# First transfers cut into halves on two queues, and re-measured durations in the plan that orders a gated-attention and expert kernel

## The chip, the cores and the metric

The kernel runs on 1 core of a Trainium2 chip. The metric is the time of one execution in device microseconds (us), and the number to predict is the median of several runs.

## The reference, cut to what matters

A gated linear attention is followed by a two-level expert layer. The attention carries a 48x48 state per batch and head through 768 tokens; the expert layer sends each of the 3072 tokens to one of 16 experts, chosen first by group and then within the group.

```python
# attention: 4 batches, 8 heads, 768 tokens, 48 wide
state = np.zeros((B, H, D, D), dtype=np.float32)
for t in range(S):
    state = alpha[:, :, t, :, None] * state + np.einsum('bhd,bhe->bhde', k[:, :, t], v[:, :, t])
    y[:, :, t] = np.einsum('bhd,bhde->bhe', q[:, :, t], state)
...
x = np.ascontiguousarray(attn_out.transpose(0, 2, 1, 3)).reshape(B * S, H * D)
# experts: x is 3072 x 384; w1 16 x 384 x 1024; w2 16 x 1024 x 384
g_idx = np.argmax(x @ w_group, axis=1)
...
e_idx = np.argmax(xg @ w_expert[g], axis=1)
h = np.maximum(xg[mask_e] @ w1[g, e], 0.0)
out[tok_idx] = combined[:, None] * (h @ w2[g, e])
```

## The kernel before

The attention works on 24 chunks of 128 tokens (6 chunks for each of 4 batches), all eight heads of a chunk at a time, as four pairs in 112 of the 128 partitions. For each chunk n there is a chain of steps. The plan names them as follows, and the profile shows them by these lines.

- `load n`: one DMA of the chunk's decays, keys, queries and values (L463), on SP's queue. Of chunks 0, 1 and 2 the parts are loaded apart: `decay0` and `decay_0` (the two halves of chunk 0's decays), `key_0`, `query_0`, `decay1`, `key_1`, `query_1`, `decay2`, then `value0`, `load2`, `value1`. Four of them go over the ACT engine's queue.
- `rev n`: a scan of the decays backward on DVE (L469, tile kd); `turn n`: a reciprocal (L475); `forth n`: a scan forward (L480, tile cq).
- `key n` and `query n`: products with keys and queries on POOL (L485 and L489, tile in or w).
- `score n`: the score matmuls on PE (L503, tile zs), masked by DVE (L512) or by an ACT copy (L517) and a POOL cut (L520).
- `turn_k n` and `kept n`: keys transposed on PE (L532, into tile zo), copied out by ACT (L537). `gain n`: matmuls (L545). `grow n`: DVE adds the old state (L554, tile sums). `scale n+1`: four ACT operations (L558, tile state).
- `own_out n` and `from n`: the output matmuls (L569, L578, tile zo); `copy n`: ACT copies them out (L584, tile yt). There is one zo tile, so `turn_k n`, which writes into it, waits for `copy n-2`.
- `row n`: matmuls (L592) that give the token rows and the expert logits. For every six chunks of the first three batches, DVE chooses the experts (from L612 to L697), and POOL sends each chunk's rows to DRAM with an indirect DMA, `scatter n` (L746).

After the attention come 18 jobs of the expert layer, with their matmuls on L281; they take the rest of the time.

What runs on each engine in which order is not written out by hand. `Plan` holds every step with its engine, a duration in us, its predecessors, and for a transfer the time from its end to its landing. `Plan.order` simulates the engines with these numbers, takes at each point the ready step with the longest remaining path, and the steps are then emitted in that order; each engine executes its list strictly in that order, whatever the real times are:

```python
soonest = max(free[e], min(early[n] for n in names))
near = [n for n in names if early[n] <= soonest + patience]
n = max(near, key=lambda m: level[m] - 2.0 * max(0.0, early[m] - soonest))
```

`warm` issues matmuls on a constant tile before the first real ones; `WARM` has their numbers (27 before chunk 0's scores, 5 behind them).

Of the kernel before, what the change touches and what calls it, by code (L numbers as in the profile page):

```python
# [19 lines left out]
ENG = mybir.EngineType  # L20
# [3 lines left out]
P = 128  # L24
# [3 lines left out]
class Plan:  # L28

    LAG = {ENG.PE: 0.2, ENG.DVE: 0.1, ENG.Activation: 0.2, ENG.Pool: 0.12, ENG.SP: 0.1}  # L30
# [80 lines left out]
def gla_then_hierarchical_moe(  # L111
# [32 lines left out]
    nc = tc.nc  # L144
# [3 lines left out]
    R = 64 + D  # L148
# [232 lines left out]
    with ExitStack() as gla:  # L381
# [323 lines left out]
        def add_send(g, b, c0, c1, counted, weighed, after_scatter):  # L705
# [51 lines left out]
            for c in range(C):  # L757
# [3 lines left out]
                plan.add(f"scatter{t0 + c}", POOL, 1.28, partial(scatter, c),  # L761
# [30 lines left out]
        WARM = (27, 5)  # L792
# [75 lines left out]
        begin("query_0", True, 0, KQ, VW)  # L868
        begin("decay1", False, 1, 0, AW)
        begin("key_1", True, 1, AW, KQ)  # L870
        begin("query_1", False, 1, KQ, VW)
        begin("decay2", True, 2, 0, AW)
        begin("value0", False, 0, VW, IW)
        begin("load2", False, 2, AW, IW)
        begin("value1", False, 1, VW, IW)
        begin("load3", False, 3)
# [38 lines left out]
        def add_decays(n):  # L915
# [6 lines left out]
            for i, (p0, p1) in enumerate(c.back):  # L922
                k = p1 - p0
                add(f"rev{n}.{i}", DVE, 0.13 + 0.273 * k, partial(back, c, p0, p1),
                    after=[src[0] if i == 0 else "decay_0", *prev, *free,
                           f"scale{n - 4}.{HP - 1}"])
                add(f"key{n}.{i}", POOL, 0.15 + 0.27 * k, partial(keys, c, p0, p1),
                    after=[f"rev{n}.{i}", src[1]])
            add(f"turn{n}", DVE, 0.18, partial(turn, c, 0, HP), after=ends_of(n, "rev", c.back))
            for i, (p0, p1) in enumerate(c.forth):  # L930
                k = p1 - p0
                add(f"forth{n}.{i}", DVE, 0.13 + 0.273 * k, partial(forth, c, p0, p1),
                    after=[f"turn{n}"])
                add(f"query{n}.{i}", POOL, 0.15 + 0.27 * k, partial(queries, c, p0, p1),
                    after=[f"forth{n}.{i}", src[2]])

        def add_scores(n):
# [8 lines left out]
            for i in range(2):  # L946
                if i < on_vector:
                    add(f"mask{i}.{n}", DVE, 0.69, partial(mask_all, c, i),
                        after=[f"score{n}", "causal", late(n - 2, "own_out")])
                    made["masked", n, i] = f"mask{i}.{n}"  # L950
                else:
                    add(f"mask{i}.{n}", ACT, 0.58, partial(mask_copy, c, i),
# [8 lines left out]
        def add_turned(n):  # L961
# [6 lines left out]
            add(f"kept{n}", ACT, 0.54, partial(kept_keys, c),  # L968
                after=[f"turn_k{n}", late(n - 2, "gain")])

        def add_rows(n):
            c = chunks[n]
            PEQ(f"row{n}", 0.87, partial(to_rows, c), after=[f"copy{n}", "wr"],
                reader=f"logit{n}")
            if in_bulk(n):
                add(f"kept_r{n}", ACT, 0.49, partial(kept_rows, c), after=[f"row{n}"])
                add(f"logit{n}", ACT, 0.25, partial(kept_logits, c), after=[f"row{n}"])
            else:
                add(f"logit{n}", DVE, 0.23, partial(logits, c), after=[f"row{n}"])
                add(f"kept_r{n}", ACT, 0.49, partial(kept_rows, c), after=[f"logit{n}"])  # L980
# [5 lines left out]
        def add_gains(n):  # L986
# [5 lines left out]
            if c.bc:  # L992
                add(f"grow{n}", DVE, 0.35, partial(grown, c),
                    after=[f"gain{n}", f"scale{n}.3", late(n - 1, "scale") and f"scale{n - 1}.3"])
            for p in range(HP):
                add(f"scale{n + 1}.{p}", ACT, 0.32, partial(scaled, chunks[n + 1], p),
# [3 lines left out]
        def add_outputs(n):  # L1000
            c = chunks[n]
            PEQ(f"own_out{n}", 0.99, partial(outputs, c),
# [4 lines left out]
            add(f"copy{n}", ACT, 0.58, partial(copied, c),  # L1007
# [368 lines left out]
    kept = []  # L1376
# [129 lines left out]
```

## Time and profile before

| what | value |
|---|---|
| median of 3 runs | 381.13 us (380.58 to 381.78) |
| the profiled execution, as timed | 380.29 us |
| its span in the profile | 378.6 us |
| PE busy, share of the span | 368.6 us, 97% |
| attention, from the first score matmul to the last job's preparation | about 7 to 122 us of the span |

The profiled execution is one run; its time is 1.69 us more than its span, and 0.84 us less than the median. PE is the engine that sets the pace; of the idle time of the others only that matters which makes PE wait.

### The profile page before, as it was taken

To read this page: it belongs to the slowest core of one execution; us is meant where nothing else is said; L and a number is where in the kernel's file an instruction comes from. 1 tells how busy PE (TensorE), PEld (TensorE's weight loads), DVE (VectorE), ACT (ScalarE), POOL (GpSimd) and SP (SyncE) were. 2 spreads that over 40 slices of the span, in tenths; PEclk is the share of its full clock that TensorE was granted. 3 is DMA by queue.
4 is the path that set the end of the run, shared out by engine and by line. 5 is a ranking of instruction groups with operands and counts; after the bars stand their busy time and mean duration, and the time that the engine had idled before them with its cause. 6 is when DMAs were issued, how large, how long until landed. Compare 5 with 4: busy or idle time off the path is not lost.

```text
span 378.6 us, 10166 instructions
## 1 busy us (share of the span) xinstructions
PE 368.6 (97%) x4122; PEld 350.4 (93%) x4122; DVE 156.7 (41%) x346; ACT 119.2 (31%) x315; POOL 200.3 (53%) x241
## 2 busy tenths in 40 slices
PE   8899999999999999999999999999999999999994
PEld 5788888888789999999999999999999999999983
DVE  6799999898976301209402022020220211201200
ACT  2666766777553121111112121121211212211210
POOL 5988779889886023526254261633525426236251
PEclk9999999999999999999999999999999999999999
DMA  8999997879883699999676576866868657655001
GB/s 291 386 402 395 410 404 259 264 249 368 317 267 131 210 331 366 348 362 344 254 227 219 190 239 242 282 217 204 243 240 294 218 197 275 260 197 192 8 22 37
DMA packets 30930, 98.08 MB, mean 259 GB/s; under 512 B 18056, under 2 KB 20036, under 8 KB 26275
## 3 DMA queue, kind: packets, MB, share of 16 engines
q1 hardware_dynamic: 25523, 86.95, 65.3%
q0 software_dynamic: 4784, 9.55, 7.4%
q10 hardware_dynamic: 576, 0.92, 0.7%
q8 instruction: 33, 0.54, 0.6%
q14 instruction: 14, 0.11, 0.1%
HBM read 85.76 MB, written 12.07 MB: 258 GB/s over the span
## 4 chain that ended last, share of the span: by engine, by line
PE 90%; POOL 3%; issue 2%; DVE 2%; DMA 1%; SPq 0%; POOLq 0%; ACT 0%; DVEq 0%
PE bank L281 63%; PE zs L503 5%; PE bank L592 5%; PE zo L569 5%; PE zo L578 3%; PE bank L545 2%; PE zs L281 2%; PE zo L532 2%; PE bank L1362 2%; DMA in<-in_rows_dram 1%; POOL in L489 1%; DVE kd L469 1%; POOL slots_d L746 1%; DVE cq L480 1%; POOL in L485 0%
## 5 line engine op out<-in xcount | busy, mean ns | idle before, releaser
L1197 POOL DMA_INDIRECT out_dram<-yq,dst_q x98 | 95.1, 971 | 146.5 <-DVE yq L1193 110.8
L281 PE MATMUL bank<-hT,w 128*64 128x96 f32 (+14 forms) x768 | 117.5, 318 | 0.0
L281 PEld LDWEIGHTS bank<-hT,w 128*128 128x128 f32 (+1 forms) x768 | 115.4, 184 | 0.0
L281 PE MATMUL bank<-xt_e,w 128*64 128x120 f32 (+14 forms) x816 | 113.5, 311 | 0.0
L281 PEld LDWEIGHTS bank<-xt_e,w 128*128 128x128 f32 (+1 forms) x816 | 111.6, 178 | 0.2 <-issue 0.2
L1240 DVE SCALAR_TENSOR_TENSOR dst_q<-xq,past_q 128x7 int32<-128x7 int32 (+1 forms) x13 | 2.2, 166 | 146.9 <-DMA out_dram<-yq,dst_q 146.9
L297 ACT ACTIVATE hT<-bank 128x192 f32<-128x192 f32 (+15 forms) x68 | 32.0, 470 | 94.8 <-PE bank L281 94.8
L308 ACT COPY yT<-bank 128x192 f32<-128x192 f32 (+28 forms) x30 | 11.9, 395 | 101.4 <-PE bank L281 101.4
L746 POOL DMA_INDIRECT slots_d<-xr,place x24 | 24.1, 1004 | 6.9 <-issue 3.8
L592 PE MATMUL bank<-wr,yt 112*64 112x116 f32 x384 | 25.3, 266 | 0.0
L1190 DVE STREAM_TRANSPOSE yq<-yT 128x672 f32<-128x672 f32 (+2 forms) x16 | 12.6, 788 | 20.2 <-ACT yT L308 20.2
L592 PEld LDWEIGHTS bank<-wr,yt 112*64 112x64 f32 x384 | 20.4, 137 | 0.4
L485 POOL TENSOR_TENSOR in<-in,kd 112x512 f32<-112x512 f32 (+1 forms) x15 | 16.7, 1116 | 5.1 <-DMA in<-in_rows_dram 2.8
L503 PE MATMUL zs<-in 48*64 48x128 f32 (+1 forms) x352 | 16.0, 275 | 2.8 <-POOL in L489 2.8
L520 POOL TENSOR_SCALAR_AFFINE_SELECT sm<-sm 128x512 f32<-128x512 f32 x27 | 16.7, 635 | 3.3 <-ACT sm L517 3.1
L584 ACT COPY yt<-zo 112x512 f32<-112x512 f32 x24 | 14.0, 585 | 14.0 <-PE zo L578 11.5
L558 ACT ACTIVATE state<-sums,kd 112x48 f32<-112x48 f32 x64 | 17.8, 331 | 1.7 <-DVE sums L554 1.7
L469 DVE TENSOR_TENSOR_SCAN kd<-in,starts 112x516 f32<-112x516 f32 (+1 forms) x15 | 17.0, 1138 | 2.9 <-DMA in<-in_rows_dram 2.8
L517 ACT COPY sm<-zs 128x512 f32<-128x512 f32 x27 | 15.4, 590 | 8.3 <-PE zs L503 7.6
L503 PEld LDWEIGHTS zs<-in 48*64 48x64 f32 (+1 forms) x352 | 13.4, 148 | 4.7 <-POOL in L489 4.0
L480 DVE TENSOR_TENSOR_SCAN cq<-in,starts 112x516 f32<-112x516 f32 (+1 forms) x16 | 17.2, 1088 | 0.8
L489 POOL TENSOR_TENSOR in<-in,cq 112x512 f32<-112x512 f32 (+1 forms) x16 | 16.9, 1060 | 0.9 <-DVE cq L480 0.7
(161 smaller groups left out, 406.9 us busy)
## 6 DMA issues: line engine op xcount, KB each, us to landing
w<-in_w_dram SPq DMA_DIRECT2D x36, 1536.0 KB, 7.1
in<-in_rows_dram SPq DMA_DIRECT2D x11, 962.5 KB, 10.4
w<-in_rows_dram SPq DMA_DIRECT2D x10, 962.5 KB, 14.5
xq<-slots_d SPq DMA_DIRECT2D x28, 85.8 KB, 9.5
slots_d<-blank SPq DMA_DIRECT2D x2, 980.0 KB
xq<-slots_d SPq DMA_DIRECT2D x24, 73.5 KB, 5.1
out_dram<-yq,dst_q POOLq DMA_INDIRECT x98
in<-in_rows_dram SPq DMA_DIRECT2D x1, 704.0 KB
```

The lines of the kernel that those rows point to most:

```text
L281: nc.tensor.matmul(z[s], lhsT=w[:, s], rhs=x, start=first, stop=last, skip_group_check=True)
L297: nc.scalar.activation(out=hT[:, f0:f0 + 2, 0:n], in_=z[:, 0:2 * n].rearrange("p (f t) -> p f t", f=2), func=AF.Relu)
L469: nc.vector.tensor_tensor_scan(out=flat(c.kd[:, p0:p1])[:, ::-1], data0=c.t[0:R, A1 * p1:A1 * p0:-1], data1=one_col.to_broadcast([R, A1 * ...
L480: nc.vector.tensor_tensor_scan(out=flat(c.cq[:, p0:p1]), data0=c.t[0:R, A1 * p0:A1 * p1], data1=starts[0:R, A1 * p0:A1 * p1], initial=1.0, ...
L485: nc.gpsimd.tensor_tensor(out=c.k[:, p0:p1], in0=c.k[:, p0:p1], in1=c.kd[:, p0:p1, 1:A1], op=ALU.mult)
L489: nc.gpsimd.tensor_tensor(out=c.q[:, p0:p1], in0=c.q[:, p0:p1], in1=c.cq[:, p0:p1, 1:A1], op=ALU.mult)
L503: nc.tensor.matmul(c.zs[i][s, p, :], lhsT=c.k[r, p, s], rhs=c.q[r, p, :], start=True, stop=True)
L558: nc.scalar.activation(out=c.st[:, p, 0:D], in_=chunks[c.n - 1].sums[:, p], func=AF.Copy, scale=c.kd[:, p, 0:1])
L569: nc.tensor.matmul(of(c.zo, p)[o], lhsT=c.v[:, h * D:h * D + o.stop - o.start], rhs=c.sm[:, i, p, :], start=(p < 2), stop=(c.bc == 0), ski ...
L592: nc.tensor.matmul(z[s, p * W:(p + 1) * W], lhsT=c.yt[:, p, s], rhs=wr[:, p, :], start=True, stop=True)
L746: sent = nc.gpsimd.indirect_dma_start(out=slots_by[t], out_offset=bass.IndirectOffsetOnAxis(ap=m["place"][:, c:c + 1], axis=0), in_=xr[:, ...
L1197: nc.gpsimd.indirect_dma_start(out=out_by.popleft().rearrange("n (j w) -> (n j) w", j=4), out_offset=bass.IndirectOffsetOnAxis(ap=dst[:, b ...
```

## The change

Three things change. The first eleven transfers are issued as two DMAs each, partitions 0 to 63 on SP's queue and the rest on ACT's queue, one transfer behind the other in order of use; of those with decays, keys and queries only the 112 partitions in use are loaded (before: 128). The durations and lags in the plan get other numbers. The number of warming matmuls ahead of chunk 0's scores is 24 instead of 27. What each step computes is as it was.

```diff
-    LAG = {ENG.PE: 0.2, ENG.DVE: 0.1, ENG.Activation: 0.2, ENG.Pool: 0.12, ENG.SP: 0.1}
+    LAG = {ENG.PE: 0.2, ENG.DVE: 0.18, ENG.Activation: 0.28, ENG.Pool: 0.2, ENG.SP: 0.1}
...
-                plan.add(f"scatter{t0 + c}", POOL, 1.28, partial(scatter, c),
+                plan.add(f"scatter{t0 + c}", POOL, 1.1, partial(scatter, c),
...
-        WARM = (27, 5)
+        WARM = (24, 5)
...
-        def begin(name, by_act, n, a=0, b=IW):
-            add(name, SP, (b - a) * P * 4 / 383.0 / 1e3,
-                partial(load, chunks[n], a, b, nc.scalar if by_act else nc.sync),
-                row="sp", lands=0.3)
+        def begin(name, n, a, b, used=P):
+
+            def halves():
+                c = chunks[n]
+                home(c)
+                for eng, z in ((nc.sync, slice(0, 64)), (nc.scalar, slice(64, used))):
+                    eng.dma_start(out=c.t[z, a:b], in_=in_d[n, z, a:b])
+
+            add(name, SP, (b - a) * used * 4 / 400.0 / 1e3, halves, row="sp", lands=0.6)
...
-        begin("decay0", False, 0, 0, HW)
-        begin("decay_0", True, 0, HW, AW)
-        begin("key_0", False, 0, AW, KQ)
...
+        begin("decay0", 0, 0, HW, R)
+        begin("decay_0", 0, HW, AW, R)
+        begin("key_0", 0, AW, KQ, R)
...
-        begin("load3", False, 3)
+        dma("load3", 0.45, partial(load, chunks[3]), IW * 512, lands=0.6)
...
-                add(f"rev{n}.{i}", DVE, 0.13 + 0.273 * k, partial(back, c, p0, p1),
+                add(f"rev{n}.{i}", DVE, 0.05 + 0.273 * k, partial(back, c, p0, p1),
```

Fourteen more durations of the plan change in the same way, twelve of them downward (an ACT copy from 0.58 to 0.48, a scale from 0.32 to 0.235).

How the queues begin, in the order of the two programs. SP's queue before, with the waits on the counters of earlier transfers (DMAHW0 to DMAHW7):

```order
L463 DMA in<-in_rows_dram 128x259
L463 DMA in<-in_rows_dram 128x512
L463 DMA in<-in_rows_dram 128x517
L463 DMA in<-in_rows_dram 128x512
L463 DMA in<-in_rows_dram 128x384 [waits DMAHW0_49]
L463 DMA in<-in_rows_dram 128x1408 [waits DMAHW1_49]
```

ACT's queue after; SP's has the same list with 64 partitions in each row, and from its fifth row on such a wait too:

```order
L864 DMA in<-in_rows_dram 48x259
L864 DMA in<-in_rows_dram 48x258
L864 DMA in<-in_rows_dram 48x512 x2
L864 DMA in<-in_rows_dram 48x517 [waits DMAHW0_49]
L864 DMA in<-in_rows_dram 48x512 [waits DMAHW2_49]
L864 DMA in<-in_rows_dram 48x512 [waits DMAHW4_49]
L864 DMA in<-in_rows_dram 48x517 [waits DMAHW6_49]
L864 DMA in<-in_rows_dram 64x384 [waits DMAHW0_49]
L864 DMA in<-in_rows_dram 64x1408 [waits DMAHW2_49]
L517 ACT_TABLE_LOAD
L517 COPY sm<-zs_200 128x512 [waits PE_49]
L537 COPY kt<-zo 128x448 [waits PE_49]
```

ACT issued four transfers ahead of its table load before, and now ten; eight counters are shared by both queues, so that a ninth transfer waits for the first one's landing, as before. An eleventh, chunk 1's values, stands behind the two copies.

DVE at chunks 3 and 4, before (kd<-w_2_281 is `rev4`, which reads what `load4` brings; sums is `grow1`):

```order
L480 SCALAR_TENSOR_TENSOR cq<-in,starts 112x516
L554 TENSOR_TENSOR sums<-state_122,bank 112x192
L469 SCALAR_TENSOR_TENSOR kd<-w_2_281,starts 112x516
L475 RECIPROCAL starts<-kd 112x4
L480 SCALAR_TENSOR_TENSOR cq<-w_2_281,starts 112x516
```

The same place after:

```order
L480 SCALAR_TENSOR_TENSOR cq<-in,starts 112x516
L469 SCALAR_TENSOR_TENSOR kd<-w_2_285,starts 112x516
L554 TENSOR_TENSOR sums<-state_122,bank 112x192
L475 RECIPROCAL starts<-kd 112x4
L480 SCALAR_TENSOR_TENSOR cq<-w_2_285,starts 112x516
```

`rev4` has moved ahead of `grow1`.

POOL near the end of the attention, before (from `key22` to `scatter15`):

```order
L485 TENSOR_TENSOR in<-in,kd 112x512
L746 DMA slots_d<-xr,place 49152x392
L489 TENSOR_TENSOR in<-in,cq 112x512
L746 DMA slots_d<-xr,place 49152x392
L485 TENSOR_TENSOR in<-in,kd 112x512
L746 DMA slots_d<-xr,place 49152x392
L489 TENSOR_TENSOR in<-in,cq 112x512
L746 DMA slots_d<-xr,place 49152x392
```

The same place after (from `key22` to `scatter15`):

```order
L485 TENSOR_TENSOR in<-in,kd 112x512
L489 TENSOR_TENSOR in<-in,cq 112x512
L746 DMA slots_d<-xr,place 49152x392 x2
L485 TENSOR_TENSOR in<-in,kd 112x512
L489 TENSOR_TENSOR in<-in,cq 112x512
L746 DMA slots_d<-xr,place 49152x392
L520 AFFINE_SELECT sm<-sm 128x512
L746 DMA slots_d<-xr,place 49152x392
```

`query22` has moved ahead of `scatter12`, and `query23` ahead of `scatter14`.

## Rows read from the trace of the kernel before

**Rows 1.** The page, part 1: busy time of PE.
```profile
PE 368.6 (97%) x4122; PEld 350.4 (93%) x4122; DVE 156.7 (41%) x346; ACT 119.2 (31%) x315; POOL 200.3 (53%) x241
```
**Rows 2.** Timeline of PE: start, us, operation; in brackets the idle time before it.
```profile
14.47 1.23 PE L503 MATMUL zs<-in 48*128 48x128 f32 x16 [0.48 <-POOL in L489]
...
19.04 1.16 PE L503 MATMUL zs<-in 48*128 48x128 f32 x16
20.13 0.60 PE L532 MATMUL zo<-ident,in 112*128 112x112 f32 x4
```
**Rows 3.** Timeline of DVE, the first five chunks.
```profile
3.63 1.27 DVE L469 TENSOR_TENSOR_SCAN kd<-in,starts 112x258 f32<-112x258 f32 x2 [1.08 <-DMA in<-in_rows_dram]
...
5.16 1.27 DVE L480 TENSOR_TENSOR_SCAN cq<-in,starts 112x258 f32<-112x258 f32 x2
7.14 1.23 DVE L469 TENSOR_TENSOR_SCAN kd<-in,starts 112x516 f32<-112x516 f32 x1 [0.71 <-DMA in<-in_rows_dram]
...
11.94 1.23 DVE L480 TENSOR_TENSOR_SCAN cq<-in,starts 112x516 f32<-112x516 f32 x1
14.20 1.23 DVE L469 TENSOR_TENSOR_SCAN kd<-in,starts 112x516 f32<-112x516 f32 x1 [1.03 <-DMA in<-in_rows_dram]
...
18.73 1.23 DVE L469 TENSOR_TENSOR_SCAN kd<-w,starts 112x516 f32<-112x516 f32 x1 [1.42 <-DMA w<-in_rows_dram]
```
**Rows 4.** Windows of the start: window, us, busy time by engine, PE clock, DMA share, GB/s.
```profile
2.00:3.00 1.00, 1.00 (x7) 0.69 (x6) 0.54 (x2) 0.27 (x1) 0.29 (x1) 1.00 0.91 257
5.00:8.00 3.00, 2.66 (x23) 1.89 (x23) 2.25 (x4) 0.00 (x0) 2.60 (x4) 1.00 1.04 387
15.00:18.70 3.70, 3.70 (x73) 3.27 (x73) 2.17 (x4) 2.64 (x8) 3.38 (x5) 1.00 1.01 408
```
**Rows 5.** DMA queues from 16.4 to 17.6 us: packets, MB, share of 16 engines.
```profile
q8 instruction: 1, 0.02, 5.7%
```
**Rows 6.** Timeline of three engines at chunks 2 to 5: from a scan to the transposes.
```profile
22.01 1.22 DVE L469 TENSOR_TENSOR_SCAN kd<-w,starts 112x516 f32<-112x516 f32 x1
23.14 0.33 DVE L554 TENSOR_TENSOR sums<-state,bank 112x192 f32<-112x192 f32 x1
...
23.50 0.56 ACT L558 ACTIVATE state<-sums,kd 112x48 f32<-112x48 f32 x2 [0.71 <-DVE sums L554]
23.97 0.56 ACT L584 COPY yt<-zo 112x512 f32<-112x512 f32 x1
...
24.63 0.60 PE L532 MATMUL zo<-ident,w 112*128 112x112 f32 x4
```
**Rows 7.** Timeline of PE, scores of chunks 22 and 23.
```profile
100.97 1.11 PE L503 MATMUL zs<-in 48*64 48x128 f32 x32 [0.63 <-POOL in L489]
...
105.75 1.21 PE L503 MATMUL zs<-in 48*64 48x128 f32 x32 [0.27 <-POOL in L489]
```
**Rows 8.** Timelines of POOL and DVE, ahead of these scores.
```profile
96.91 1.18 POOL L485 TENSOR_TENSOR in<-in,kd 112x512 f32<-112x512 f32 x1
98.69 1.01 POOL L746 DMA_INDIRECT slots_d<-xr,place  x1 [0.61 <-DVE xr L697]
99.73 1.18 POOL L489 TENSOR_TENSOR in<-in,cq 112x512 f32<-112x512 f32 x1
...
104.51 1.18 POOL L489 TENSOR_TENSOR in<-in,cq 112x512 f32<-112x512 f32 x1
...
96.40 1.22 DVE L480 TENSOR_TENSOR_SCAN cq<-in,starts 112x516 f32<-112x516 f32 x1
...
101.13 1.23 DVE L480 TENSOR_TENSOR_SCAN cq<-in,starts 112x516 f32<-112x516 f32 x1
```
**Rows 9.** Timeline of PE at the start: warming matmuls, and the scores behind a gap.
```profile
1.29 5.46 PE L409 MATMUL bank<-nothing 128*128 128x256 bf16 x27 [1.29 <-DVE nothing L844]
...
10.58 1.16 PE L503 MATMUL zs<-in 48*128 48x128 f32 x16 [1.06 <-POOL in L489]
```
**Rows 10.** Windows behind the last matmul, in the columns of rows 4.
```profile
373.20:376.00 2.80, 0.00 (x0) 0.00 (x0) 0.00 (x0) 0.36 (x1) 0.94 (x1) 1.00 0.17 51
376.00:378.60 2.60, 0.00 (x0) 0.00 (x0) 0.00 (x0) 0.00 (x0) 0.00 (x0) 0.92 0.04 9
```

More of the change, by code (lines that the diff above doesn't have):

```diff
@@ L947, in add_scores @@
                 if i < on_vector:
-                    add(f"mask{i}.{n}", DVE, 0.69, partial(mask_all, c, i),
+                    add(f"mask{i}.{n}", DVE, 0.6, partial(mask_all, c, i),
                         after=[f"score{n}", "causal", late(n - 2, "own_out")])
@@ L951, in add_scores @@
                 else:
-                    add(f"mask{i}.{n}", ACT, 0.58, partial(mask_copy, c, i),
+                    add(f"mask{i}.{n}", ACT, 0.48, partial(mask_copy, c, i),
                         after=[f"score{n}", late(n - 2, "own_out")])
@@ L967, in add_turned @@
                 + ends_of(n, "key", c.back))
-            add(f"kept{n}", ACT, 0.54, partial(kept_keys, c),
+            add(f"kept{n}", ACT, 0.43, partial(kept_keys, c),
                 after=[f"turn_k{n}", late(n - 2, "gain")])
@@ L972, in add_rows @@
             c = chunks[n]
-            PEQ(f"row{n}", 0.87, partial(to_rows, c), after=[f"copy{n}", "wr"],
+            PEQ(f"row{n}", 0.78, partial(to_rows, c), after=[f"copy{n}", "wr"],
                 reader=f"logit{n}")
             if in_bulk(n):
-                add(f"kept_r{n}", ACT, 0.49, partial(kept_rows, c), after=[f"row{n}"])
-                add(f"logit{n}", ACT, 0.25, partial(kept_logits, c), after=[f"row{n}"])
+                add(f"kept_r{n}", ACT, 0.38, partial(kept_rows, c), after=[f"row{n}"])
+                add(f"logit{n}", ACT, 0.15, partial(kept_logits, c), after=[f"row{n}"])
             else:
                 add(f"logit{n}", DVE, 0.23, partial(logits, c), after=[f"row{n}"])
-                add(f"kept_r{n}", ACT, 0.49, partial(kept_rows, c), after=[f"logit{n}"])
+                add(f"kept_r{n}", ACT, 0.38, partial(kept_rows, c), after=[f"logit{n}"])
             also[f"logit{n}"] = f"kept_r{n}"
@@ L992, in add_gains @@
             if c.bc:
-                add(f"grow{n}", DVE, 0.35, partial(grown, c),
+                add(f"grow{n}", DVE, 0.26, partial(grown, c),
                     after=[f"gain{n}", f"scale{n}.3", late(n - 1, "scale") and f"scale{n - 1}.3"])
             for p in range(HP):
-                add(f"scale{n + 1}.{p}", ACT, 0.32, partial(scaled, chunks[n + 1], p),
+                add(f"scale{n + 1}.{p}", ACT, 0.235, partial(scaled, chunks[n + 1], p),
                     after=[f"grow{n}" if c.bc else f"gain{n}", f"rev{n + 1}.0", "states0",
@@ L1001, in add_outputs @@
             c = chunks[n]
-            PEQ(f"own_out{n}", 0.99, partial(outputs, c),
+            PEQ(f"own_out{n}", 1.04, partial(outputs, c),
                 after=[made["masked", n, 0], made["masked", n, 1], late(n - 1, "copy"),
@@ L1006, in add_outputs @@
                 PEQ(f"from{n}", 0.47 if QUARTERS <= n + 1 < NT else 0.59, partial(from_before, c), after=[f"scale{n}.3"])
-            add(f"copy{n}", ACT, 0.58, partial(copied, c),
+            add(f"copy{n}", ACT, 0.48, partial(copied, c),
                 after=[f"from{n}" if c.bc else f"own_out{n}", late(n - 2, "row")])
```

24 lines of the change are left out of this document (12 added, 12 removed).

## The prediction

> **What bounds the kernel now.** The page comes first: PE is busy for 368.6 of 378.6 us [rows 1], so a change pays only where it shortens a time in which PE has nothing to do or warms up on constants. The timeline of PE shows where that is. From the scores of chunk 2 at 14.47 us on, PE runs without a pause over the rest of the attention, but for 0.63 and 0.27 us ahead of the scores of chunks 22 and 23, where it waits for a POOL product [rows 2, 7]. Two things are thus to be had: the stretch up to 14.47 us, and these 0.90 us. All else is matmuls that the change leaves as they are.
>
> The timeline of DVE then says what the first stretch waits for. DVE starts four of its first scans late, each for a transfer: at 3.63, 7.14, 14.20 and 18.73 us, after 1.08, 0.71, 1.03 and 1.42 us without work [rows 3]. The last is `rev4`, so `load4` had landed at 18.7. While it waited, PE was not idle: its scores of chunk 3 began at 19.04 and the transposes of `turn_k3` at 20.13 [rows 2]. The transfers have no pause of their own there; all 16 DMA engines are busy, and move 387 GB/s from 5 to 8 us and 408 GB/s from 15 to 18.7 us [rows 4].
>
> **The start, step by step.** The first halves move 116 KB in place of the 265 KB that the two queues carried side by side, so chunk 0's first scan should start earlier than 3.63 us; I take 3.1, since its issue and its way to the first byte stay as they are, with 3.63 (no gain) and 2.7 as bounds. Behind it DVE works for 2.80 us without a wait (3.63 to 5.16 + 1.27 = 6.43), and now goes straight on to chunk 1 if `decay1` has landed at 5.9. It should: 0.92 MB lie up to its end, which at 387 GB/s take 2.4 us from about 2 us on. From `rev1` to the end of `forth2` DVE needed 6.03 us without a pause (7.14 to 11.94 + 1.23), and `score2` began 1.30 us behind that. So `score2` comes at 3.1 + 2.8 + 6.0 + 1.3 = 13.2 in place of 14.47 us: 1.2 us gained at this point, and `score3` begins at 17.8.
>
> The three warming matmuls that go are time in which PE waits anyway. The ACT table load now stands behind ten issues, the last of which waits for an early landing; I expect it done by 8 us, when chunk 0's mask is ready to be copied. If it were 1 us later, a POOL cut would be, which has that room before chunk 0's outputs. The second half of chunk 1's values, behind two ACT copies, is issued near 9 us and is needed near 15 us. Both cost nothing; either without its cover would cost part of the 1.2 us.
>
> **What is late next.** The new order puts `rev4` ahead of `grow1` on DVE. DVE's list is strict, so whatever stands behind `rev4` waits for `load4`: first `grow1`; behind it `scale2` and `copy1` on ACT; behind `copy1`, through the one zo tile, `turn_k3` on PE, and behind that all of PE. So everything hangs on one landing. Before, 18.73 us. Now 16 of 128 partitions of the first eight transfers (3599 columns of 4 bytes, 230 KB) are no longer moved ahead of it, at 387 to 408 GB/s 0.57 us: `load4` at 18.16 us. I take no more from the two queues, since the engines were full with one. Inside this landing there is a packet of instructions that took 5.7% of 16 x 1.2 us, or 1.09 us, on one of the engines [rows 5]; whether it again hits the engine that finishes last, I can't say, and without it the landing is 17.1. The other bound: halves keep only half the bytes in flight under the same eight counters; if that costs a pause, up to 0.5 us, it is 18.7.
>
> From the landing to the transposes the same chain stands elsewhere with nothing else in it: a scan at 22.01, `grow2` to 23.47, two scales and the copy to 24.53, transposes at 24.63 [rows 6], 2.62 us. So `turn_k3` moves from 20.13 to 18.16 + 2.62 = 20.78 us: 0.65 us **later** than before, with PE idle from 18.9 on. The 1.2 us of the start are gone, and more. `rev5` wants `load5` 2.9 us behind `load4`; 0.99 MB at 408 GB/s take 2.4, so nothing more is lost there.
>
> **The end of the attention.** Before, `query22` stood behind `scatter12`, which waited 0.61 us for a DVE result, and began at 99.73, though `key22` had ended at 98.09 and the scan at 97.62. In the new order it follows `key22` at once: 98.1 to 99.3, where PE is ready for it at 100.97 - 0.63 = 100.34. `query23` now has two scatters ahead of it (2 x 1.18 us), then `key23` (1.19): it ends near 104.1, where PE is ready at 105.48 [rows 7, 8]. Both waits go, with over 1 us to spare: 0.90 us gained. The price if the cover is gone is these 0.90 us again, no more.
>
> **The sum.** + 0.65 - 0.90 = - 0.25 us: 380.29 becomes 380.04. The profiled execution lies 0.84 us under the median, so in terms of the median 380.9 us.
>
> **Weighed against the skill.** The table of rows 4 shows the engines full whichever queue issues. The Trainium skill, "DMA: Bandwidth & Descriptors", under "Bandwidth", goes further and speaks against halves: it advises to gather transfers to a MiB, and calls those under 64 KB bound by their descriptors, with 138 GB/s at 64 KB (measured there with GpSimd as the issuer). By its figure the 1.61 MB of the first eight pairs would be an estimated 11.7 us; by the row at 387 GB/s they are 4.2 us. I go by the row, since several transfers are in flight at once and the rows in them are as long as before; what is left of the rule is the second rival.
>
> **Rivals.** *The landing is early.* If the packet of instructions falls on another engine, and the lagging engine lags less, `load4` lands at 17.2 us or before. Each 0.1 us counts fully, down to 16.3, from where `turn_k3` follows `score3` at 18.9 without a wait. Then 1.23 + 0.90 = 2.13 us are gained: 379.0. For it: the last engine's time is made of that one packet and of chance; against: the packet was there before. Faster by over 0.3% (1.14 us, about what a measurement of this kernel can tell from no change) it is from a landing before 17.3.
>
> *The halves move slowly.* In the first us of transfers, with short rows and small pieces, 257 GB/s were moved in place of 387 [rows 4]. If all halves, 1.61 MB, go at that rate, they take 6.3 us instead of 4.2: `load4` comes 2.1 us later, at 20.2, and PE's pause grows with it, to + 2.75 - 0.90 = + 1.85 us: 383.0. It is slower by over 0.3% from a landing past 19.6. Against it: the rate had risen to 387 before these transfers were over, in rows as short as these.
>
> *PE's clock falls in the new pause.* PE stands still for 1.9 us, from 18.9 to 20.8. A pause of 1.06 us left the granted clock at 1.00, the level of 2.4 GHz [rows 9]; behind the last matmul it was still at 1.00 up to 376.0, and lower, at a mean of 0.92, only after that [rows 10]. So 2.8 us without a matmul left it as it was, and I give the fall little. If it comes, matmuls run at 1.2 GHz until PE has worked for a time; the 27 warming matmuls took 5.46 us, and half of that, 2.7 us, bounds the price: 383.6. The Trainium skill, "TensorE: Matmul & The Clock Gate", Part 1, has the array fall back to half rate after an idle stretch; by that rule the pause matters, and rows 10 show that a longer one was borne here.
>
> *The change doesn't do what it says.* Two queues feed the same 16 engines; if no transfer lands sooner, `score2` stays at 14.47, `load4` at 18.73, `turn_k3` comes at 21.35, + 1.22 - 0.90 = + 0.3 us: 381.5. This ends as no change, since the new order of DVE and POOL acts all the same.
>
> **Chances and numbers.** Landing between 17.3 and 19.6, with the end's gain: 0.61, the rival without effect among it; it gives 379.8 to 382.2 us. An early landing: 0.25. Slow halves 0.08, the clock 0.04, and another stall of the new order that I don't see 0.02. So faster 0.25, same 0.61, slower 0.14. The prediction is 380.9 us. The range leaves out about one in ten on each side: 379.2 lies just above the full gain, and 382.4 just past the forecast's own end.
>
> **What would show it.** In the profile after, the first scan should start near 3.1 us, `score2` near 13.2. `rev4` should show an idle time of over 2 us that a DMA ended, at about 18.2, and `turn_k3` should follow it by 2.6 us, with PE idle ahead of it for nearly 2 us. The scores of chunks 22 and 23 should have no wait for POOL. The prediction is wrong if `rev4` starts before 17.3 or after 19.6 us, if the granted clock falls near 20 us, or if PE waits at a place of the attention where it didn't before, other than `turn_k3`.

## The result: 384.3 us, slower by 0.9%

| | kernel before | changed kernel |
|---|---|---|
| median, 6 runs each | 380.62 us (380.29 to 381.78) | 384.26 us (383.09 to 384.69) |
| ratio, 95% interval | | 1.0087 (1.0067 to 1.0107) |
| span of the profiled execution | 378.6 us | 382.3 us |

The prediction was 380.9 us, no change, with a range up to 382.4; it was wrong. The span grew by 3.7 us. PE is busy for 2.4 us more (368.6 in [rows 1], now 371.0) with fewer instructions, so part of its work ran slower. On the page after, the line of PE, then the granted clock in tenths and the GB/s for each fortieth of the span (9.6 us):

```profile
PE 371.0 (97%) x4119; PEld 352.4 (92%) x4119; DVE 157.2 (41%) x346; ACT 119.7 (31%) x315; POOL 200.6 (52%) x241
...
PEclk9699999999999999999999999999999999999999
...
GB/s 192 303 418 388 408 426 255 265 266 307 401 185 233 122 307 377 360 360 359 277 273 213 200 217 210 280 239 236 218 219 298 237 196 252 279 206 190 8 22 37
```

The first two slices differ: 192 and 303 GB/s (291 and 386 before), and a clock of 0.6 in the second (0.9 or more before). So the loss lies at the start. The scans on DVE after, which answer to [rows 3], show how:

```profile
3.15 0.69 DVE L469 TENSOR_TENSOR_SCAN kd<-in,starts 112x258 f32<-112x258 f32 x1 [0.60 <-DMA in<-in_rows_dram]
4.68 0.69 DVE L469 TENSOR_TENSOR_SCAN kd<-in,starts 112x258 f32<-112x258 f32 x1 [0.84 <-DMA in<-in_rows_dram]
...
7.52 1.23 DVE L469 TENSOR_TENSOR_SCAN kd<-in,starts 112x516 f32<-112x516 f32 x1 [0.61 <-DMA in<-in_rows_dram]
...
17.39 1.23 DVE L469 TENSOR_TENSOR_SCAN kd<-in,starts 112x516 f32<-112x516 f32 x1 [3.85 <-DMA in<-in_rows_dram]
...
21.86 1.23 DVE L469 TENSOR_TENSOR_SCAN kd<-w,starts 112x516 f32<-112x516 f32 x1 [1.68 <-DMA w<-in_rows_dram]
23.00 0.33 DVE L554 TENSOR_TENSOR sums<-state,bank 112x192 f32<-112x192 f32 x1
```

The first scan is half a microsecond earlier than before, every one behind it is later: `rev1` at 7.52 (before 7.14), `rev3` at 17.39 (14.20), `rev4` at 21.86 (18.73), all three at the end of a wait for a DMA. The windows after, in the columns of [rows 4] (clock, DMA share and GB/s are the last three):

```profile
2.00:3.00 1.00, 1.00 (x7) 0.67 (x6) 0.54 (x2) 0.00 (x0) 0.29 (x1) 1.00 0.62 161
5.00:8.00 3.00, 1.72 (x10) 0.91 (x9) 2.32 (x5) 0.04 (x1) 2.14 (x4) 1.00 0.94 260
...
9.00:12.00 3.00, 2.65 (x22) 1.99 (x22) 2.99 (x4) 1.27 (x3) 2.97 (x4) 0.64 0.95 249
12.00:15.00 3.00, 3.00 (x34) 2.50 (x33) 1.42 (x2) 1.46 (x3) 0.81 (x1) 0.50 1.03 253
15.00:18.70 3.70, 3.70 (x49) 3.12 (x48) 1.27 (x2) 2.33 (x8) 2.68 (x4) 0.77 1.03 375
```

260 GB/s in place of 387 from 5 to 8 us, and no better up to 15 us, although the engines show a share of 0.94 to 1.03. SP's queue is late as well; its DMA issues before, then after:

```profile
0.84 5.15 SPq L463 DMA_DIRECT2D in<-in_rows_dram  x8
```
```profile
0.84 9.05 SPq L864 DMA_DIRECT2D in<-in_rows_dram  x11
9.94 0.68 SPq L463 DMA_DIRECT2D in<-in_rows_dram  x1
```

Before, `load3` was the last of eight issues that were over at 5.99 us; after, it is issued at 9.94. PE after, which answers to [rows 2]:

```profile
7.87 1.35 PE L503 MATMUL zs<-in 48*128 48x128 f32 x16 [1.28 <-POOL in L489]
...
10.96 2.18 PE L503 MATMUL zs<-in 48*128 48x128 f32 x16 [0.35 <-POOL in L489]
...
16.76 1.16 PE L503 MATMUL zs<-in 48*128 48x128 f32 x16
...
21.48 1.23 PE L503 MATMUL zs<-in 48*128 48x128 f32 x16 [0.16 <-POOL in L489]
24.45 0.60 PE L532 MATMUL zo<-ident,in 112*128 112x112 f32 x4 [1.74 <-ACT yt L584]
```

`score1` takes 2.18 us: the granted clock is at 0.50, the level of 1.2 GHz, from about 10 us to nearly 17. `turn_k3` comes at 24.45 in place of 20.13, 4.3 us late, with PE idle for 1.74 us ahead of it. At the end of the attention the two waits of [rows 7] are gone, but a new one of 0.63 us stands ahead of the counting of chosen experts:

```profile
100.05 0.20 PE L773 MATMUL bank<-picked,before 128*128 128x96 bf16 x1 [0.63 <-DVE sums L554]
...
105.34 1.07 PE L503 MATMUL zs<-in 48*64 48x128 f32 x32
...
109.63 1.08 PE L503 MATMUL zs<-in 48*64 48x128 f32 x32
```

The scores of chunk 23 are 3.88 us late (105.75 in [rows 7]), so the piece between gave back 0.44 of the 4.32 us; the 0.2 us from there to the 3.7 of the span are spread too thin to name.

### The profile page after: what moved, and what is told of

Read it like the earlier page. It is cut to its first block, busy times and chain, and to the rows that moved or that the text cites. A ratio compares the mean times of both kernels' runs of the same rounds, so it can differ in the third digit from the quotient of the medians.

```text
span 382.3 us, 10166 instructions
## 1 busy us (share of the span) xinstructions
PE 371.0 (97%) x4119; PEld 352.4 (92%) x4119; DVE 157.2 (41%) x346; ACT 119.7 (31%) x315; POOL 200.6 (52%) x241
## 4 chain that ended last, share of the span: by engine, by line
PE 88%; DMA 7%; issue 2%; DVE 1%; SPq 1%; ACT 0%; POOLq 0%; POOL 0%; DVEq 0%
PE bank L281 63%; PE bank L592 5%; PE zs L503 4%; PE zo L569 4%; DMA in<-in_rows_dram 4%; DMA w<-in_rows_dram 3%; PE zo L578 3%; PE bank L545 2%; PE zs L281 2%; PE zo L532 2%; PE bank L1367 2%; PE bank L781 0%; SPq L864 0%; DVE kd L469 0%; DVE lg L612 0%
## 5 line engine op out<-in xcount | busy, mean ns | idle before, releaser
L503 PE MATMUL zs<-in 48*64 48x128 f32 (+1 forms) x352 | 16.8, 281 | 1.8 <-POOL in L489 1.8
L503 PEld LDWEIGHTS zs<-in 48*64 48x64 f32 (+1 forms) x352 | 14.4, 154 | 3.7 <-POOL in L489 3.3
## 6 DMA issues: line engine op xcount, KB each, us to landing
xq<-slots_d SPq DMA_DIRECT2D x28, 85.8 KB, 11.7
```

The source lines that it names most:

```text
L503: nc.tensor.matmul(c.zs[i][s, p, :], lhsT=c.k[r, p, s], rhs=c.q[r, p, :], start=True, stop=True)
```

## The experiments

Each ratio is to runs of the kernel before on the same chip, with its 95% interval. It is not the quotient of the two medians; a difference of medians, as given in us below, can lie up to 0.7 us from what the ratio says.

**Whole transfers in the new plan.** In `halves` of the changed kernel:

```diff
-                for eng, z in ((nc.sync, slice(0, 64)), (nc.scalar, slice(64, used))):
-                    eng.dma_start(out=c.t[z, a:b], in_=in_d[n, z, a:b])
+                eng = nc.scalar if name in ("decay_0", "query_0", "key_1", "decay2") else nc.sync
+                eng.dma_start(out=c.t[:, a:b], in_=in_d[n, :, a:b])
```

> The changed kernel with its plan, its order and its 24 warming matmuls, but the first eleven transfers are issued as in the kernel before: one DMA each over all 128 partitions, alternately on SP and ACT. Theory A (the halves move slowly): the landings of the kernel before come back, so the scan of chunk 4 starts at 18.7 us and the transposes of chunk 3 follow at 21.3, 1.2 us later than in the kernel before (20.13). In the changed kernel these transposes came 4.3 us late and its span was 3.7 us longer, so everything behind them is worth -0.6; here 380.6 + 1.2 - 0.6 = 381.2 us. Theory B (the new order of the plan costs the time, the transfers cost little): as the changed kernel, 384 us.

Measured: 380.80 us, 0.9994 (0.9973 to 1.0016). The scan of chunk 4 began even earlier than expected. From its windows and timelines:

```profile
6.00:9.00 3.00, 2.07 (x24) 1.80 (x25) 1.69 (x3) 0.65 (x2) 1.53 (x4) 1.00 1.06 401
9.00:12.00 3.00, 1.25 (x20) 1.00 (x17) 2.96 (x5) 0.38 (x1) 3.00 (x4) 1.00 1.03 413
```
```profile
17.59 1.23 DVE L469 TENSOR_TENSOR_SCAN kd<-w,starts 112x516 f32<-112x516 f32 x1 [0.19 <-DMA w<-in_rows_dram]
```
```profile
34.14 0.60 PE L532 MATMUL zo<-ident,w 112*128 112x112 f32 x4 [0.46 <-ACT yt L584]
```

All of the loss is in how the first transfers are issued, none that can be measured in the plan (theory A; B falls). This run takes back both the halves and the 112 partitions; the two are taken apart further below. The new plan is no gain either: in this profile chunk 2's scores came at 15.00 us, and its order has a wait of 0.46 us of its own, at chunk 6, which the changed kernel, late as it is, doesn't have. The profiled execution took 1.2 us more than the median; it has a pause of 1.49 us inside the scores of chunk 22 that nothing in the profile explains.

**Halves in the old plan.** `begin` of the kernel before issues the two halves of the changed kernel; its numbers, its order and 27 warming matmuls stay.

```diff
...
-                partial(load, chunks[n], a, b, nc.scalar if by_act else nc.sync),
+                partial(load, chunks[n]) if name == "load3" else halves,
```

> The kernel before with its own plan numbers, order and 27 warming matmuls; only the first eleven transfers are halved as in the changed kernel (64 partitions on SP, 48 or 64 on ACT). Theory A (halves are slow): chunk 4 lands near 21.8 us in place of 18.7; its scan stands behind the growing of chunk 1 here, so the transposes of chunk 3 don't wait for it, but the scores of chunk 4 do: 21.8 + 4.1 (from the scan's start to the end of the product with queries before) + 0.1 = 26.0 in place of 23.53 us. That is +2.5: 383.1 us. Theory B (the order): 380.6 us, no change.

Measured: 384.37 us, 1.0089 (1.0058 to 1.0119). Theory A, with 1.3 us more than its figure. Chunk 4's scan began at 21.56, as expected, but its scores at 26.83 and not 26.0, and not for a landing: behind the scores of chunk 2 (17.03) PE had no pause up to them, and the clock was 0.50 from 12 to 18 us.

```profile
17.03 1.97 PE L503 MATMUL zs<-in 48*128 48x128 f32 x16
...
26.83 1.16 PE L503 MATMUL zs<-w 48*128 48x128 f32 x16
```

Two things were thus late together: the transfers, and PE's own work.

**The growing of chunk 1 first.**

```diff
                     after=[src[0] if i == 0 else "decay_0", *prev, *free,
-                           f"scale{n - 4}.{HP - 1}"])
+                           f"scale{n - 4}.{HP - 1}", "grow1" if n == 4 else None])
```

> The changed kernel with one more edge in the plan: the scan of chunk 4 comes after the growing of chunk 1 on DVE, as in the kernel before; the halves stay. If the strict order of DVE turns the late landing into the wait of 1.74 us ahead of the transposes of chunk 3, this wait goes and they follow the scores of chunk 3 at 22.6. Then the scores of chunk 4 come at 26.0, bound by the landing at 21.8 and by PE's own work alike, in place of 27.86: -1.9, 382.4 us. If the order costs nothing beside the landing: 384 us.

Measured: 383.81 us, 1.0072 (1.0046 to 1.0097); the wait of 1.74 us is gone, but the 1.9 us did not come:

```profile
7.85 2.15 PE L503 MATMUL zs<-in 48*128 48x128 f32 x16 [2.33 <-DMA in<-in_rows_dram]
...
22.25 1.16 PE L503 MATMUL zs<-in 48*128 48x128 f32 x16
```

The clock fell from the start of chunk 0's scores here, and PE worked without a pause until those of chunk 3 at 22.25. So chunk 4's scores came at 26.74, 1.1 us earlier than in the changed kernel and not 1.9: right behind the wait for the landing stood PE's own work at half clock. The time fell by 0.45 us, which the two intervals don't tell from nothing.

**The same with more warming.** 30 warming matmuls in place of 24, and 12 in place of 5.

```diff
-        PEQ("warm0", 0.166 * WARM[0], partial(warm, WARM[0]), after=["nothing"])
+        PEQ("warm0", 0.166 * WARM[0], partial(warm, 30), after=["nothing"])
...
```

> The run with the growing of chunk 1 ahead of the scan of chunk 4 on DVE, with 30 warming matmuls in place of 24 ahead of chunk 0's scores and 12 in place of 5 behind its transposes; the rest and its order stay. In that run the granted clock was 0.50 from about 8 to 17 us, and PE had no pause from 7.85 us to the scores of chunk 3 at 22.25. If PE at half clock is what sets these scores, the matmuls from 30 warming ones hold the clock and the scores come when chunk 3's product with queries is ready, 17.59 + 3.85 = 21.4: 0.8 us gained, 383.0 us. If the late transfers alone set them: 383.8 us.

Measured: 384.26 us, 1.0076 (1.0049 to 1.0104): no gain. The clock was held to nearly 20 us; what PE waited for meanwhile were transfers, and behind these pauses the clock fell after all (0.50 from 21 to 24 us):

```profile
9.00:12.00 3.00, 2.98 (x33) 2.49 (x31) 1.64 (x3) 1.06 (x3) 2.85 (x4) 1.00 1.00 244
```
```profile
17.07 1.23 PE L503 MATMUL zs<-in 48*128 48x128 f32 x16 [2.01 <-POOL in L489]
...
21.33 0.96 PE L545 MATMUL bank<-in,kt 128*64 128x48 f32 x15 [2.50 <-DMA in<-in_rows_dram]
```

The last wait is for the values of chunk 1, whose half on ACT stands behind two copies. This profiled execution is the longest of its runs (387.02 us), so its waits show what can happen, not what usually does.

**Even and odd partitions.** In the changed kernel:

```diff
-                for eng, z in ((nc.sync, slice(0, 64)), (nc.scalar, slice(64, used))):
-                    eng.dma_start(out=c.t[z, a:b], in_=in_d[n, z, a:b])
+                for eng, i in ((nc.sync, 0), (nc.scalar, 1)):
+                    eng.dma_start(out=c.t[i:P:2, a:b], in_=in_d[n, i:P:2, a:b])
```

> The changed kernel, but each of the first eleven transfers is halved in another way: SP moves the even and ACT the odd partitions, 64 each (128 are moved, the changed kernel moved 112 of the first eight). Number of DMAs, their sizes, the length of their rows, the two queues and the waits on the eight counters stay. Theory A1 (what is slow is a DMA whose rows lie in one half of the partitions): from 3 to 9 us about 380 GB/s are moved in place of the 250 of the changed kernel, the scan of chunk 4 starts near 18.7, and the time is near 381.2 us. Theory A2 (twice as many transfers of half the size, under eight counters, keep too few bytes in flight): 250 GB/s again, the scan of chunk 4 at 21.9 or later, 384 us or more. The Trainium skill, 'SBUF - State Buffer', 'Can I just issue two DMAs to hit both halves?', denies that two transfers on partitions 0 and 64 reach the rate of one over all 128; by it A1 is right.

Measured: 388.84 us, 1.0199 (1.0164 to 1.0234). Neither theory's case: 266 GB/s from 3 to 6 us, 291 from 6 to 9, and then

```profile
9.00:12.00 3.00, 3.00 (x23) 2.10 (x19) 2.93 (x6) 1.41 (x2) 1.93 (x3) 0.58 0.47 117
```

The engines had nothing to move: the program makes the odd and even pieces of the values wait for the products on POOL too, which the expectation had overlooked. This run says nothing on the disputed point; the pair further below takes it up again.

**Halves by columns.**

```diff
-                for eng, z in ((nc.sync, slice(0, 64)), (nc.scalar, slice(64, used))):
-                    eng.dma_start(out=c.t[z, a:b], in_=in_d[n, z, a:b])
+                for eng, i, j in ((nc.sync, a, (a + b) // 2), (nc.scalar, (a + b) // 2, b)):
+                    eng.dma_start(out=c.t[:, i:j], in_=in_d[n, :, i:j])
```

> The changed kernel, but each of the first eleven transfers is halved by its columns: SP moves the first half of the columns of all 128 partitions, ACT the second. The number of DMAs, the two queues and the waits on the eight counters stay as in the changed kernel, but every DMA now spans all partitions, with rows half as long. Rate while busy, as GB/s divided by the DMA share, from 6 to 9 us: 390 in the kernel before, 262 in the changed one, 342 with even and odd partitions. Theory A1 (a DMA within half of the partitions is what moves slowly): 340 or more while busy from 6 us on, the scan of chunk 4 at 18.7 us, the time near that of whole transfers, 381 us. Theory A2 (too few bytes in flight under eight counters): while busy the rate is whole, but the share of busy time falls under 0.9, the scan of chunk 4 comes at 20 or later, 383 to 384 us.

Measured: 382.76 us, 1.0055 (1.0033 to 1.0077), the scan of chunk 4 at 20.08. The time is A2's nearly, the share isn't: 0.99, 0.94, 0.96 with 288, 287 and 283 GB/s from 3 to 12 us. Rows half as long may have a part in it, so the next run was made.

**Useless small transfers beside whole ones.**

```diff
...
+                eng.dma_start(out=c.t[:, a:b], in_=in_d[n, :, a:b])
+                i = len(extra)
+                extra.append(other.dma_start(out=spare[0:16, 8 * i:8 * i + 8],
+                                             in_=in_d[n, 0:16, a:a + 8]))
```

> The changed kernel with whole transfers over 128 partitions; beside each of the eleven the other queue issues a useless DMA of 512 bytes into a spare tile. So the number of DMAs, their division between the two queues and the waits on the eight counters are those of the changed kernel, while rows and partitions are those of the kernel before. Theory A2 (twice as many DMAs under eight counters leave too few bytes in flight): the DMA share falls under 0.9 somewhere from 3 to 12 us, the scan of chunk 4 comes at 19.5 to 20.5 us as with halves by columns, and the time is 382 to 383 us. If the number of DMAs costs nothing: a share of 1.0 throughout, the scan of chunk 4 between 17.6 and 18.7, 380.8 us.

Measured: 383.19 us, 1.0055 (1.0031 to 1.0078), the scan of chunk 4 at 20.64. Windows, and the scans of chunks 3 and 4:

```profile
3.00:6.00 3.00, 3.00 (x16) 2.13 (x15) 2.74 (x5) 0.00 (x0) 0.76 (x2) 1.00 0.90 274
6.00:9.00 3.00, 2.14 (x22) 1.42 (x21) 1.67 (x3) 0.98 (x1) 2.32 (x4) 1.00 0.88 284
9.00:12.00 3.00, 2.19 (x27) 1.77 (x26) 2.92 (x5) 1.46 (x4) 2.62 (x4) 1.00 0.79 213
```
```profile
17.73 1.23 DVE L469 TENSOR_TENSOR_SCAN kd<-in,starts 112x516 f32<-112x516 f32 x1 [4.44 <-DMA in<-in_rows_dram]
...
20.64 1.23 DVE L469 TENSOR_TENSOR_SCAN kd<-w,starts 112x516 f32<-112x516 f32 x1
```

Theory A2, with a falling share. Eleven transfers of 512 bytes cost 2.2 us. Chunk 4's scan had no wait of its own; it is late because chunk 3's had waited 4.44 us for its landing. That follows the issue of `load3` on SP's queue, with whole transfers alone and then with the small ones:

```profile
5.37 0.45 SPq L463 DMA_DIRECT2D in<-in_rows_dram  x1
```
```profile
8.59 0.43 SPq L463 DMA_DIRECT2D in<-in_rows_dram  x1
```

From this issue to chunk 3's scan it took as long in both (9.24 and 9.14 us). Ahead of it the queue waited 3.0 us for earlier landings (1.3 with whole transfers alone), and its four small issues took 1.7 us; so the counters and the issuing both have a part in the late issue. The first scan began at 3.09 us, so that gain needs no halves.

**112 partitions, whole.** As the first run, but `c.t[0:used, a:b]`.

```diff
-                eng.dma_start(out=c.t[:, a:b], in_=in_d[n, :, a:b])
+                eng.dma_start(out=c.t[0:used, a:b], in_=in_d[n, 0:used, a:b])
```

> The changed kernel with whole transfers on alternate queues, as in the run with whole transfers, but of the first eight only the 112 partitions in use are moved. The prediction's step by bytes: 0.23 MB less, the scan of chunk 4 0.57 us earlier than with 128 partitions (17.59 us there, so 17.0), and 380.5 us. The rival: a DMA of 112 partitions, 7 rows for each of 16 engines, runs into itself. In the kernel before, the only one of that shape, wr, ran beside load3 from 12 to 15 us, and there the 16 engines were full but moved 318 GB/s in place of 413. Then the first eight move at some 318, 1.4 MB in 4.4 us in place of the 4.0 that 1.6 MB took at 400: the scan of chunk 4 comes 0.4 us later, 381.2 us.

Measured: 381.41 us, 1.0024 (1.0004 to 1.0043), the scan of chunk 4 at 18.61 in place of 17.59. Fewer bytes, and no earlier than with 128 (17.59, and 18.73 in the kernel before). The rate from 6 to 9 us goes with it:

```profile
6.00:9.00 3.00, 2.42 (x24) 1.70 (x23) 0.86 (x2) 0.41 (x1) 1.75 (x3) 1.00 1.09 268
```
```profile
18.61 1.23 DVE L469 TENSOR_TENSOR_SCAN kd<-w,starts 112x516 f32<-112x516 f32 x1 [0.17 <-DMA w<-in_rows_dram]
```

268 GB/s at a full share, against 401 with 128 partitions at the same place. Here the engines are never short of work; what is in flight moves slowly. The interval leaves open how much of it reaches the time.

**Only the first eight in halves**, lower and upper, or even and odd, 64 partitions each:

```diff
...
+                parts = ((nc.sync, slice(0, 64)), (nc.scalar, slice(64, P))) if used < P else ((nc.sync, slice(0, P)),)
...
```

> The changed kernel, but only the first eight transfers are halved (partitions 0 to 63 on SP, 64 to 127 on ACT, 128 partitions moved in place of 112), and the values of chunks 0 and 1 and the rest of chunk 2 come whole on SP. To be read beside the next run, which differs from it in nothing but which 64 partitions a half has. Theory A1 (a DMA within one half of the partitions moves slowly): from 6 to 9 us the rate while busy (GB/s divided by the DMA share) is again near 262, as in the changed kernel. The scan of chunk 4 comes near 19.5 us, the time near 382.3.

> As the run before it, with even partitions on SP and odd ones on ACT. Products on POOL wait here for all pieces of their chunk, which the other run doesn't have, so its time says less than its rate. Theory A1: 340 or more while busy from 6 to 9 us, the scan of chunk 4 at 19.0 or earlier. If it doesn't matter which partitions a half has: 262 again and 19.5.

Measured: 384.70 us, 1.0090 (1.0061 to 1.0119) for lower and upper; 383.33 us, 1.0054 (1.0032 to 1.0075) for even and odd. From 6 to 9 us 277 and 311 GB/s at shares of 0.95 and 0.91, so 292 and 342 while busy; but from 3 to 6 us 251 and 232, and chunk 4's scan at 20.97, without a wait, and at 21.54. Both scans later than either theory gave; unclear. The time of the first says one thing plainly: halves over all 128 partitions lose as much as the changed kernel, so its 112 partitions aren't needed for the loss.

**Halves that are large.** The first eight transfers joined to five, so that halves are ten DMAs and not sixteen.

```diff
+                if name in ("decay_0", "query_0", "query_1"):
+                    return
+                to = {"decay0": AW, "key_0": VW, "key_1": VW}.get(name, b)
+                parts = ((nc.sync, slice(0, 64)), (nc.scalar, slice(64, P)))
...
```

> The changed kernel with its first eight transfers joined to five (decays, keys with queries, decays, keys with queries, decays), each halved as partitions 0 to 63 on SP and 64 to 127 on ACT, and whole transfers behind them. So there are ten DMAs of halves in place of sixteen, 132 to 262 KB each, and nothing of them waits for a landing but the last pair; the partitions of a half are those of the changed kernel. Theory A2 alone (the number of DMAs is all that costs): the DMA share is 1.0 and the rate 350 to 410 GB/s from 3 to 9 us, as with whole transfers; the scan of chunk 4 at 17.6 to 18.7 us, 381 to 381.5 us. With theory A1 beside it (a half moves slowly whatever its size): a full share, but 260 to 310 GB/s from 3 to 9 us, the scan of chunk 4 past 19 us, 382 us or more.

Measured: 388.84 us, 1.0148 (1.0110 to 1.0187; the kernel before ran at 382.68 us on this chip). Windows and PE:

```profile
3.00:6.00 3.00, 3.00 (x17) 2.04 (x15) 1.91 (x4) 1.28 (x1) 0.00 (x0) 1.00 1.00 251
6.00:9.00 3.00, 0.25 (x2) 0.25 (x4) 1.59 (x3) 0.00 (x0) 2.26 (x4) 0.94 1.03 265
9.00:12.00 3.00, 3.00 (x23) 2.62 (x24) 2.93 (x6) 0.78 (x2) 2.45 (x4) 0.50 1.03 352
```
```profile
8.75 2.08 PE L503 MATMUL zs<-in 48*128 48x128 f32 x16 [2.75 <-POOL in L489]
...
27.65 1.16 PE L503 MATMUL zs<-w 48*128 48x128 f32 x16
```

A full share and 251 to 265 GB/s: ten DMAs of halves move no faster than the changed kernel's twenty-two (258 GB/s from 3 to 6 us, 246 from 6 to 9), so halves of the partitions are slow by themselves (A1 beside A2). But chunk 4 was there by 18.66 us, since the whole transfers behind were held up less (`load3` was issued at 8.59, in the changed kernel at 9.94); so the scan was not past 19, and yet the time is one of the two worst. PE stood for 2.75 us, then the clock was at 0.50, and PE had no further pause up to chunk 4's scores.

**The same with more warming**, 36 and 10 matmuls in place of 24 and 5.

```diff
-        PEQ("warm0", 0.166 * WARM[0], partial(warm, WARM[0]), after=["nothing"])
+        PEQ("warm0", 0.166 * WARM[0], partial(warm, 36), after=["nothing"])
...
```

> The run with five joined transfers in halves, with 36 warming matmuls in place of 24 ahead of chunk 0's scores and 10 in place of 5 behind its transposes; nothing else. In that run chunk 4 landed by 18.7 us, but PE paused 2.75 us ahead of chunk 0's scores, the granted clock was 0.50 from 9 to 18 us, and PE had no pause from 8.75 us on, so that the scores of chunk 4 began at 27.65. If the half clock sets that, the longer warming leaves the clock at 1.00, the scores of chunk 3 begin at 15.86 + 3.85 + 0.1 = 19.8 us and those of chunk 4 at 24.3, 3.3 us earlier, and the ratio falls from 1.0148 by 0.9%, to 1.006. If the clock is not what is waited for: 1.013 to 1.017 again.

Measured: 381.84 us, 1.0027 (1.0003 to 1.0051), lower than expected. The clock stayed at 1.00 from 2 to 21 us:

```profile
20.22 1.23 DVE L469 TENSOR_TENSOR_SCAN kd<-w,starts 112x516 f32<-112x516 f32 x1 [0.81 <-DMA w<-in_rows_dram]
```
```profile
16.18 1.23 PE L503 MATMUL zs<-in 48*128 48x128 f32 x16 [0.40 <-POOL in L489]
20.74 1.21 PE L503 MATMUL zs<-in 48*128 48x128 f32 x16
22.81 0.60 PE L532 MATMUL zo<-ident,in 112*128 112x112 f32 x4 [0.85 <-ACT yt L584]
...
26.21 1.16 PE L503 MATMUL zs<-w 48*128 48x128 f32 x16
```

Chunk 3's scores came 2.4 us earlier than without the warming (20.74 instead of 23.15), chunk 4's only 1.4 us (26.21 instead of 27.65), because its landing, at 20.22 in this execution, was now what PE waited for. The ratio fell by 0.0121, 4.6 us. The start accounts for 1.4 of that in the two profiles; where the rest is from isn't settled, as the run without the warming lost time behind the attention's start too, on a chip that was slower in itself. That the half clock costs time where the transfers aren't late is shown; how much lies between 1.4 and 4.6 us.

**The two scatters alone.** In the kernel before, ahead of the emission:

```diff
+        for late, first in (("scatter12", "query22.0"), ("scatter14", "query23.0")):
+            done.remove(late)
+            done.insert(done.index(first) + 1, late)
```

> The kernel before with one thing of the changed one: in the order that the plan emits, scatter12 stands behind query22 and scatter14 behind query23 on POOL; nothing else moves. If the two waits for POOL ahead of the scores of chunks 22 and 23 (0.63 and 0.27 us) go and nothing takes their place, 0.90 us are gained: 379.7 us, a ratio of 0.9976. If another engine is due at the same point, as in the changed kernel, where the piece behind the scores of chunk 4 was only 0.6 us shorter than before: 380.0 us.

Measured: 379.90 us against 380.75, 0.9982 (0.9962 to 1.0002). Both waits of [rows 7] are gone in its profile, and 0.85 us of the 0.90 show in the median (0.7 by the ratio), though the interval just reaches 1. It is the lowest median of all kernels here.

**Chunk 1's decays earlier, on top of that.** `key_0` goes over ACT and `key_1` over SP.

```diff
-        begin("key_0", False, 0, AW, KQ)
+        begin("key_0", True, 0, AW, KQ)
...
```

> The kernel before with the two scatters moved behind the query products as in the earlier run, and the queues' shares of the first eight whole transfers changed: SP issues decay0, decay1, key_1, query_1, ACT decay_0, key_0, query_0, decay2. The decays of chunk 1, second on SP in place of third, land near 5 us, so its scan follows chunk 0's without the wait of 0.71 us. If DVE sets the scores of chunk 2, they come 0.5 to 0.7 us earlier than 14.5, and the time is 379.9 - 0.5 = 379.4 us. If POOL does, because the queries of chunk 0 now land third, near 7 us in place of 5.1, nothing is gained: 379.9 us or more.

Measured: 382.24 us (379.53 to 389.78), 1.0015 (0.9991 to 1.0038). The scan of chunk 1 began at 6.22 without a wait, but:

```profile
8.39 1.95 PE L506 MATMUL zs<-in 48*128 48x128 f32 x16 [2.11 <-POOL in L492]
```

Chunk 0's queries were late, its scores came 1.3 us later than before, and the clock was 0.50 from 9 to 12 us. The rival held, and behind the pause the clock fell as well.

## Why the prediction was wrong, by its own steps

- **The first scan at 3.1 us**: right (3.15). It needs no halves (3.09 with whole transfers and small ones between).
- **`decay1` landed at 5.9, by 0.92 MB at 387 GB/s, and `score2` at 13.2**: wrong, 7.52 and 16.76. The rate of [rows 4] was that of whole transfers over 128 partitions, and was applied to others.
- **`load4` at 18.16: the step that failed.** It was 21.86, 3.7 us later than the term said, and all that hangs on it moved along. Three parts of the step were wrong. "The engines were full with one" queue took a full share for a full rate: at shares of 0.99 to 1.09 the engines moved between 244 and 413 GB/s in the rows above. The 0.57 us by bytes are not to be had: without 16 of the partitions 268 GB/s are moved where 401 were, and the landing is no earlier. And the bound for the eight counters, up to 0.5 us, was guessed and not read; with the small transfers chunk 3 landed at 17.73, 3.1 to 3.5 us behind the three profiles with whole transfers alone (14.20, 14.39, 14.61) and as late as in the changed kernel (17.39), and the time is 2.2 us longer. Of the 3.6 us of the changed kernel that number of DMAs alone gives 2.2 (2.0 with halves by columns); for the partitions of the halves 1.4 remain, if the two add up, which no run shows by itself.
- **The chain of 2.62 us from `rev4` to `turn_k3`**: right, 2.59 (21.86 to 24.45), through these two rows of ACT:

```profile
23.37 0.56 ACT L558 ACTIVATE state<-sums,kd 112x48 f32<-112x48 f32 x2 [2.85 <-DVE sums L554]
23.83 0.56 ACT L584 COPY yt<-zo 112x512 f32<-112x512 f32 x1
```

- **`rev4` ahead of `grow1`**: it made the wait where the prediction said, but undoing it gave 0.45 us of the 3.6, no more than the intervals leave open. With the transfers as they were, the whole new order cost nothing measurable.
- **The two covers at the start**: the ACT table load ended at 9.24 and not by 8, but the scores whose copy stood behind it ended at 9.22; the second half of chunk 1's values was issued at 10.09, a microsecond late. Neither shows as a wait of PE, in a kernel that other landings had made late.
- **The end, -0.90**: the waits went, and alone they are worth 0.85 us by the medians, with an interval that just reaches none; in the changed kernel the 0.63 us ahead of the counting took most of it back.
- **The rival "the halves move slowly"** was the right one, at a chance of 0.08, with the condition (a landing past 19.6) that it named. Its 383.0 us were 1.3 too low: it slowed only the halves themselves, up to about 8 us, while 250 GB/s lasted to 15 us. The reason it was put low, that rows as short had reached 387, looked at the length of rows and not at how many partitions or how many DMAs.
- **The rival of the clock** put the fall into the pause ahead of `turn_k3`; that pause, 1.74 us, left it at 1.00 from 21 to 27 us. It fell near 10 us instead, behind a pause of 1.28 us ahead of chunk 0's scores, with 16 score matmuls, 4 transposes and 5 warming ones in between. What that fall costs in the changed kernel no run shows: the clock was held only with the growing of chunk 1 put first, where nothing was gained, with late transfers as the next wait. Where the landing was early it cost at least 1.4 us; whether the bound of 2.7 holds is open.

The Trainium skill, "SBUF — State Buffer", under "Can I just issue two DMAs to hit both halves?", says that two transfers on the two halves of the partitions nearly serialize, and that all ports are reached only by one transfer over all 128. The rows of the large halves (251 and 265 GB/s at full share) agree with it in direction. The Trainium skill, "DMA: Bandwidth & Descriptors", under "Bandwidth", which the prediction weighed, advises against small transfers. The run with the useless ones shows a price of their number, 2.2 us; but the estimate of 11.7 us that the prediction worked out from its figure for the first eight pairs was too long: the last of them, the decays of chunk 2, were scanned from 10.78 us of the span on, and the transfers had begun at about 2.

## What to carry to other kernels

A busy share of DMA engines is not a rate: before a transfer is cut, look for rows of transfers of the same shape, partitions and number, and count the transfers against the counters that they share. Where several limits lie close together at the start (landings, a strict queue, the clock of PE), taking one away shows the next, and a gain has to be worked out against that one. A cheap move at a place where PE visibly waits (here two scatters) may be worth more than a rearranged start.

## What was not expected of the hardware

- With the same first transfers, the scan of chunk 4 began at 18.73 us in the kernel before, 17.59 in the first experiment and 18.95 with the two scatters moved: landings differ by over a microsecond between these single executions. Whether that is chance, or the other order of the first experiment, is open.
- The clock did not fall behind pauses of 1.58 and 1.75 us of PE in the run with whole transfers, and fell behind one of 1.28 us in the changed kernel. What tells these apart is open.
